# The attention's biases of the first 31 items on GpSimd, with omega scaled as it is loaded

## The chip, the cores and the metric

One core of a Trainium2 chip runs the kernel. The metric is the device time of one execution in microseconds, the median of several runs. The engines are TensorE (PE, with PEld for its weight loads), VectorE (DVE), ScalarE (ACT), GpSimd (POOL) and SyncE (SP), which issues the loads.

## The reference

Three layers follow one another: a linear attention with random features, a two-layer network, and a layer of 8 experts of which each token uses one.

```python
scale = 1.0 / np.sqrt(np.sqrt(D))                  # D = 64
def phi(x):                                        # x = q * scale or k * scale
    proj = np.einsum('bhsd,md->bhsm', x, omega)    # 128 features
    sq = np.sum(x * x, axis=-1, keepdims=True) / 2.0
    h = proj - sq
    h = h - np.max(h, axis=-1, keepdims=True)
    return np.exp(h) / np.sqrt(m)
kv = np.einsum('bhsm,bhsd->bhmd', k_p, v); z = np.sum(k_p, axis=2)
num = np.einsum('bhsm,bhmd->bhsd', q_p, kv)
den = np.einsum('bhsm,bhm->bhs', q_p, z)[..., None] + 1e-06
x = num / den                                      # (4, 8, 576, 64) -> (2304, 512)
h = x @ w_in; y = np.maximum(0.01 * h, h) @ w_out  # 512 -> 2048 -> 512
# experts: argmax of y @ w_gate; relu(y @ w1[e]) @ w2[e], scaled by two gates
```

Everything is float32; the matrix products of the last two layers are made of three products of split numbers.

## The kernel before

The attention's work is cut into 74 items: 36 of keys and 38 of queries, each of four tiles of 128 rows (three in some). An item goes through stages, one per tick of a software pipeline: load, squares, projection, phi, and then either the product with the values (keys) or transposes, the product with the keys' sums, and the division (queries). The list `seq` sets the order of the items; `turn` counts them. The first 13 are 9 items of keys and 4 of queries, with the loading of the first weights between them; the first 31 end with the first queries of the second batch.

From about 50 us on, the two-layer network runs between the stages: for every block of 256 tokens (`c`) and every eighth of the hidden width (`u`) a unit `h_unit` (24 products, lines 463 to 465) and a unit `x_unit` (12 products, lines 482 to 484). Blocks 0 and 1 run side by side. Their weights come as 64-bit words and are turned into float32 on the way (`load_w`, 32 times in the first 170 us): ScalarE takes one part (line 201), VectorE three steps (202 to 204), ScalarE casts the high half (209), GpSimd subtracts for the low half (`wil`, `wol`, line 212). From about 170 us on the weights are resident.

What phi does for one item: TensorE projects into PSUM (`pw`, line 290, with `om_raw`); VectorE takes the maximum `mx` over the 128 features (302, or 304 and 305); `ngm` and `bias` (309, 311) follow on VectorE; ScalarE makes four exponentials (319) with `bias` as their bias. `s2` is half the sum of squares: in 9 items TensorE makes it from `sq` (265, 280), in all others GpSimd squares the rows (`nat`, 270), VectorE sums them (`ssq`, 271) and GpSimd scales them (273). The tiles `mx`, `ngm`, `bias`, `s2` and `ssq` have two buffers each.

```python
ngm = att.tile([P, 4], F32, name="ngm", tag="ngm")
nc.vector.scalar_tensor_tensor(ngm[:, 0:nt], mx[:, 0:nt], -sc, s2[:, 0:nt], op0=ALU.mult, op1=ALU.add)
bias = att.tile([P, 4], F32, name="bias", tag="bias")
nc.vector.tensor_sub(bias[:, 0:nt], ngm[:, 0:nt], s2[:, 0:nt])
```

Each engine runs its instructions in one fixed order. A scheduler sets that order when the program is built, by its own estimates of what each instruction costs, so a change of an engine or an operation can reorder the others around it.

Of the kernel before, what the change touches and what calls it, by code (L numbers as in the profile page):

```python
# [15 lines left out]
AF = mybir.ActivationFunctionType  # L16
ALU = mybir.AluOpType
# [27 lines left out]
WFROM = 0  # L45
WU = 6
TAIL = 9
KQ = 8
WARM = 8
NSLOT = NTOK // SLOT - 1  # L50
# [37 lines left out]
def tile_kernel(ctx: ExitStack, tc: tile.TileContext, kT, k_nat, v_nat, qT, q_nat, om, w_in, w_out, wg, w1, w2, out, stop=None, dbg=None):  # L88
    nc = tc.nc
    sc = 1.0 / math.sqrt(math.sqrt(HD))  # L90
# [44 lines left out]
    with ExitStack() as pa:  # L135
# [9 lines left out]

        om_raw = const.tile([P, 2 * M], F32, name="om_raw")
        nc.sync.dma_start(om_raw, om)
        halves = const.tile([P, 2], F32, name="halves")
        nc.vector.memset(halves, 0.0)
        for i in range(2):  # L150
# [142 lines left out]
        def phi(st, nt):  # L293
            pj = st["pj"]
            if not dense[0] and st["turn"] % 2 == 0:
                h = sb.tile([P, 4, M], F32, name="h", tag="gh")
            else:
                h = att.tile([P, 4, M], F32, name="h", tag="h", bufs=3)
            mx = att.tile([P, 4], F32, name="mx", tag="mx")
            o = mx.rearrange("p (h j) -> p j h", h=2)  # L300
            if nt == 4:
                nc.vector.tensor_reduce(o, pj.rearrange("p (j h) m -> p j h m", h=2), axis=AX.X, op=ALU.max)
            else:
                nc.vector.tensor_reduce(o[:, 0, :], pj[:, 0:2, :], axis=AX.X, op=ALU.max)
                nc.vector.tensor_reduce(o[:, 1, 0:1], pj[:, 2:3, :], axis=AX.X, op=ALU.max)

            s2 = st["s2"]
            ngm = att.tile([P, 4], F32, name="ngm", tag="ngm")
            nc.vector.scalar_tensor_tensor(ngm[:, 0:nt], mx[:, 0:nt], -sc, s2[:, 0:nt], op0=ALU.mult, op1=ALU.add)
            bias = att.tile([P, 4], F32, name="bias", tag="bias")  # L310
            nc.vector.tensor_sub(bias[:, 0:nt], ngm[:, 0:nt], s2[:, 0:nt])  # L311
            st["phi"] = h, pj.rearrange("p (j h) m -> p h j m", h=2), bias
            if st["tight"]:
                phi2(st, nt)

        def phi2(st, nt):
            h, src, bias = st["phi"]
            for j in range(nt):
                nc.scalar.activation(h[:, j, :], src[:, j // 2, j % 2], AF.Exp, bias=bias[:, j:j + 1], scale=sc)  # L319
            st["e"] = h  # L320

        def k_item(b, g):
# [18 lines left out]
            def s_phi():  # L341
                if big:
                    st["vb"] = groups["v", first][:, at - first]
                else:
                    st["vb"] = att.tile([P, 5 * HV], F32, name="vb", tag="vb")
                    n = (5 if any((g * 4 + j) % PT == 0 for j in range(4)) else 4) * HV
                    nc.sync.dma_start(st["vb"][:, 0:n], v_nat[at, :, 0:n])
                phi(st, 4)

            def s_kv():  # L350
                o = 0
                for j in range(4):
# [7 lines left out]
                    if w == PT - 1:  # L360
                        kv_done(b, p)

            st["phi2"] = lambda: phi2(st, 4)
            st["stages"] = [s_load, s_split, s_proj, s_phi, st["phi2"], s_kv]
            return -1, st["stages"]
# [12 lines left out]
        def q_item(b, i, pair0, np_, tile0, at, grp):  # L378
# [16 lines left out]
            def s_phi():  # L395
                phi(st, nt)
# [27 lines left out]
            def s_xt():  # L424
# [18 lines left out]
                if rest_:  # L443
                    o = t[0:HD, np_ * per:np_ * (per + P)].rearrange("p (a k l) -> p a k l", a=np_, k=2)
                    for k in range(2):
                        at = (slice(k * HD, (k + 1) * HD), slice(pair0, pair0 + np_), slice(off + per, off + L))
                        hi_lo(xh[at], xl[at], o[:, :, k, :], nc.scalar, nc.vector)

            st["phi2"] = lambda: phi2(st, nt)
            st["stages"] = [s_load, s_split, s_proj, s_phi, st["phi2"], s_tr, s_num, s_xt]  # L450
            return c, st["stages"]
# [155 lines left out]
        def q_items(b, i):  # L607
            L = pieces(b)[i][1]
            np_ = pairs_of(L)
            first = sum(n for _, n in pieces(b)[:i]) * NH // P  # L610
            at = sum(NH // 2 // pairs_of(n) for c in range(b + 1) for _, n in pieces(c)[:i if c == b else None])
            n = NH // 2 // np_
            return [q_item(b, i, j * np_, np_, first + j * np_ * 2 * L // P, at + j, (at + j // 2 * 2, min(2, n - j // 2 * 2), False)) for j in range(n)]

        def k_items(b, g0, g1):
            return [k_item(b, g) for g in range(g0, g1)]


        seq = k_items(0, 0, KQ) + q_items(0, 0) + k_items(0, KQ, 9)
        first = len(seq)  # L620
# [187 lines left out]
        for i, (c, u) in enumerate(pairs):  # L808

            rate = RATE  # L810
            for cc in range(c, NCH):
                left = [k + TAIL for k, it in enumerate(seq) if it[0] == cc] + [len(o) for c_, o in flow if c_ == cc]
                if left and hbeg.get(cc, 0) - 1 > i:
# [170 lines left out]
```

## Time and profile before

| | us |
|---|---|
| median of 3 runs | 886.59 |
| lowest and highest run | 882.37 and 889.65 |
| the profiled execution | 887.9 |
| its span, first to last instruction | 886.2 |
| TensorE busy in the span | 840.5 |
| VectorE | 449.8 |
| ScalarE | 307.0 |
| GpSimd | 179.5 |

The profile is of one execution. An engine counts as busy while an instruction runs, stalls within it included; a wait for a semaphore counts as idle. TensorE's matmuls overlap, so its busy time is not its best time. PEclk is the share of full clock that the throttle granted.

### The profile page before, as it was taken

To read this page: it belongs to the slowest core of one execution; us is meant where nothing else is said; L and a number is where in the kernel's file an instruction comes from. 1 tells how busy PE (TensorE), PEld (TensorE's weight loads), DVE (VectorE), ACT (ScalarE), POOL (GpSimd) and SP (SyncE) were. 2 spreads that over 40 slices of the span, in tenths; PEclk is the share of its full clock that TensorE was granted. 3 is DMA by queue.
4 is the path that set the end of the run, shared out by engine and by line. 5 is a ranking of instruction groups with operands and counts; after the bars stand their busy time and mean duration, and the time that the engine had idled before them with its cause. 6 is when DMAs were issued, how large, how long until landed. Compare 5 with 4: busy or idle time off the path is not lost. (4 is left out here: it accounts for less than half of the span.)

```text
span 886.2 us, 13999 instructions
## 1 busy us (share of the span) xinstructions
PE 840.5 (95%) x5299; PEld 734.0 (83%) x5299; DVE 449.8 (51%) x1142; ACT 307.0 (35%) x755; POOL 179.5 (20%) x253
## 2 busy tenths in 40 slices
PE   9889998999999999999999999997996999999996
PEld 7768777798899899988889899876886779888894
DVE  6899879626545445445554444454335433512220
ACT  4666655424324224323322232142125432411210
POOL 3545544301221012122010010120013211220001
PEclk9899999999999999999999999999999999999998
DMA  7636554301542021152020000155026622410001
GB/s 225 209 116 192 189 179 138 123 1 31 74 108 78 2 43 53 35 97 60 19 43 6 1 25 1 36 186 72 1 94 208 204 80 98 150 54 21 10 24 33
DMA packets 46153, 73.55 MB, mean 83 GB/s; under 512 B 6017, under 2 KB 28673, under 8 KB 46082
## 3 DMA queue, kind: packets, MB, share of 16 engines
q1 hardware_dynamic: 42562, 63.14, 25.7%
q0 software_dynamic: 3520, 9.47, 3.4%
q8 instruction: 44, 0.72, 0.4%
q14 instruction: 27, 0.22, 0.1%
HBM read 62.00 MB, written 10.59 MB: 82 GB/s over the span
## 5 line engine op out<-in xcount | busy, mean ns | idle before, releaser
L463 PE MATMUL hp<-xh,wih 128*128 128x256 f32 x576 | 167.2, 290 | 2.3 <-DVE xl L212 2.0
L464 PE MATMUL hp<-xl,wih 128*128 128x256 f32 x576 | 162.7, 282 | 0.1
L465 PE MATMUL hp<-xh,wil 128*128 128x256 f32 x576 | 162.1, 281 | 0.0
L482 PE MATMUL acc<-woh,gh 128*128 128x512 f32 x288 | 123.8, 430 | 1.4 <-ACT kv L373 1.4
L484 PE MATMUL acc<-woh,gl 128*128 128x512 f32 x288 | 116.6, 406 | 6.8 <-DVE gl L212 6.8
L319 ACT ACTIVATE h<-pw,bias 128x128 f32<-128x128 f32 x288 | 84.8, 372 | 107.5 <-DVE bias L311 87.7
L469 DVE SCALAR_TENSOR_TENSOR g<-hp,g 128x512 f32<-128x512 f32 x72 | 49.6, 689 | 130.7 <-ACT g L468 118.8
L483 PE MATMUL acc<-wol,gh 128*128 128x512 f32 x288 | 114.8, 399 | 0.0
L463 PEld LDWEIGHTS hp<-xh,wih 128*128 128x128 f32 x576 | 109.7, 190 | 5.5 <-issue 2.4
L464 PEld LDWEIGHTS hp<-xl,wih 128*128 128x128 f32 x576 | 109.6, 190 | 2.2 <-DVE xl L212 0.3
L465 PEld LDWEIGHTS hp<-xh,wil 128*128 128x128 f32 x576 | 109.5, 190 | 0.0
L468 ACT COPY g<-hp 128x512 f32<-128x512 f32 x72 | 42.2, 586 | 134.2 <-PE hp L465 129.6
L713 PE MATMUL eht<-exh,ewh 128*128 128x256 f32 (+1 forms) x256 | 76.9, 301 | 8.9 <-DVE ehl L717 7.2
L714 PE MATMUL eht<-exl,ewh 128*128 128x256 f32 (+1 forms) x256 | 76.4, 298 | 0.4 <-DVE exl L212 0.4
L715 PE MATMUL eht<-exh,ewl 128*128 128x256 f32 (+1 forms) x256 | 76.0, 297 | 0.0
L290 PE MATMUL pw<-om_raw,xpair 128*128 128x256 f32 (+1 forms) x260 | 72.0, 393 | 2.3 <-ACT h L319 2.3
L270 POOL TENSOR_TENSOR nat<-nat 128x256 f32<-128x256 f32 (+1 forms) x65 | 44.8, 692 | 136.8 <-DMA nat<-k_nat 59.0
L484 PEld LDWEIGHTS acc<-woh,gl 128*128 128x128 f32 x288 | 54.9, 191 | 20.5 <-DVE gl L212 8.4
L212 DVE TENSOR_TENSOR ewl<-eraw,ewh 128x1024 fp32r<-128x1024 f32 x32 | 39.1, 1225 | 59.9 <-ACT ewh L209 49.8
L482 PEld LDWEIGHTS acc<-woh,gh 128*128 128x128 f32 x288 | 54.6, 190 | 12.9 <-ACT kv L373 1.8
L730 PE MATMUL eyt<-ewh,ehh 128*128 128x512 f32 (+1 forms) x160 | 64.3, 402 | 0.6 <-ACT ehh L716 0.6
L731 PE MATMUL eyt<-ewl,ehh 128*128 128x512 f32 (+1 forms) x160 | 63.4, 396 | 0.0
(157 smaller groups left out, 1470.9 us busy)
## 6 DMA issues: line engine op xcount, KB each, us to landing
eraw<-w SPq DMA_DIRECT2D x32, 512.0 KB, 4.0
wraw<-w_in SPq DMA_DIRECT2D x16, 512.0 KB, 6.1
wraw<-w_out SPq DMA_DIRECT2D x16, 512.0 KB, 3.4
x_d<-rows SPq DMA_DIRECT2D x9, 514.0 KB
xpair<-qT SPq DMA_DIRECT2D x18, 256.0 KB, 9.0
nat<-q_nat SPq DMA_DIRECT2D x30, 128.0 KB, 2.6
nat<-k_nat SPq DMA_DIRECT2D x27, 128.0 KB, 2.6
xpair<-kT SPq DMA_DIRECT2D x12, 256.0 KB, 3.4
```

What stands on the lines that cost most here:

```text
L290: nc.tensor.matmul(pj[:, 2 * j:2 * j + k // HD, :], st["raw"][0:k, j * P:(j + 1) * P], om_raw[0:k, 0:M * k // HD], start=True, stop=True)
L319: nc.scalar.activation(h[:, j, :], src[:, j // 2, j % 2], AF.Exp, bias=bias[:, j:j + 1], scale=sc)
L463: nc.tensor.matmul(hp[:, i, :], a, xh[:, d, :], start=d == 0, stop=False)
L464: nc.tensor.matmul(hp[:, i, :], a, xl[:, d, :], start=False, stop=False)
L465: nc.tensor.matmul(hp[:, i, :], b_, xh[:, d, :], start=False, stop=d == ND - 1)
L482: nc.tensor.matmul(acc[t], a, h_, start=u == 0 and i == 0, stop=False)
L483: nc.tensor.matmul(acc[t], a, l_, start=False, stop=False)
L484: nc.tensor.matmul(acc[t], b_, h_, start=False, stop=u == NU - 1 and i == 1)
L713: nc.tensor.matmul(t, wh, self.xh[:, d, 0:n], start=d == 0, stop=False)
L714: nc.tensor.matmul(t, wh, self.xl[:, d, 0:n], start=False, stop=False)
L715: nc.tensor.matmul(t, wl, self.xh[:, d, 0:n], start=False, stop=d == ND - 1)
L730: nc.tensor.matmul(t, a, wh, start=f == 0, stop=False)
```

## The change

`om_raw` is multiplied once by the scale, on VectorE, as soon as it has landed. The projections and their maxima then come out scaled, so `ngm` needs no factor: it becomes s2 - mx, a plain subtraction, and the exponentials lose their scale. For the items with `turn` below 31, `ngm` and `bias` are made on GpSimd; for the other 43 they stay on VectorE.

```diff
--- before.py
+++ after.py
@@ -45,6 +45,7 @@
 WFROM = 0
 WU = 6
 TAIL = 9
+EARLY = 31
 KQ = 8
 WARM = 8
 NSLOT = NTOK // SLOT - 1
@@ -145,6 +146,7 @@
 
         om_raw = const.tile([P, 2 * M], F32, name="om_raw")
         nc.sync.dma_start(om_raw, om)
+        nc.vector.tensor_scalar_mul(om_raw, om_raw, sc)
         halves = const.tile([P, 2], F32, name="halves")
         nc.vector.memset(halves, 0.0)
         for i in range(2):
@@ -305,10 +307,11 @@
                 nc.vector.tensor_reduce(o[:, 1, 0:1], pj[:, 2:3, :], axis=AX.X, op=ALU.max)
 
             s2 = st["s2"]
+            eng = nc.gpsimd if st["turn"] < EARLY else nc.vector
             ngm = att.tile([P, 4], F32, name="ngm", tag="ngm")
-            nc.vector.scalar_tensor_tensor(ngm[:, 0:nt], mx[:, 0:nt], -sc, s2[:, 0:nt], op0=ALU.mult, op1=ALU.add)
+            eng.tensor_sub(ngm[:, 0:nt], s2[:, 0:nt], mx[:, 0:nt])
             bias = att.tile([P, 4], F32, name="bias", tag="bias")
-            nc.vector.tensor_sub(bias[:, 0:nt], ngm[:, 0:nt], s2[:, 0:nt])
+            eng.tensor_sub(bias[:, 0:nt], ngm[:, 0:nt], s2[:, 0:nt])
             st["phi"] = h, pj.rearrange("p (j h) m -> p h j m", h=2), bias
             if st["tight"]:
                 phi2(st, nt)
@@ -316,7 +319,7 @@
         def phi2(st, nt):
             h, src, bias = st["phi"]
             for j in range(nt):
-                nc.scalar.activation(h[:, j, :], src[:, j // 2, j % 2], AF.Exp, bias=bias[:, j:j + 1], scale=sc)
+                nc.scalar.activation(h[:, j, :], src[:, j // 2, j % 2], AF.Exp, bias=bias[:, j:j + 1])
             st["e"] = h
 
         def k_item(b, g):
```

In all, 31 pairs leave VectorE for GpSimd, one instruction is added on VectorE, and nothing else changes in number. The order that the scheduler makes changes around them. The names' numbers are one higher in the change, since it has one more instruction.

VectorE, where the first queries' phi begins: `mx_451` is the maximum of an item, `bias_455` its bias; `w32_381` is a weight block in its three steps, `mx_485` and `mx_530` belong to the next two items. Before:

```order
L309 SCALAR_TENSOR_TENSOR ngm_428<-mx_426,s2_352 128x4
L311 TENSOR_TENSOR bias_401<-ngm_399,s2_357 128x4
L202 TENSOR_SCALAR w32_381<-w32_381 128x512
L311 TENSOR_TENSOR bias_430<-ngm_428,s2_352 128x4
L302 TENSOR_REDUCE mx_451<-pw_422 128x2x2
L203 SCALAR_TENSOR_TENSOR w32_381<-wraw_379,w32_381 128x512
L271 TENSOR_REDUCE ssq_417<-nat_415 128x4
L204 SCALAR_TENSOR_TENSOR w32_381<-wraw_379,w32_381 128x512
L309 SCALAR_TENSOR_TENSOR ngm_453<-mx_451,s2_391 128x4
L302 TENSOR_REDUCE mx_485<-pw_447 128x2x2
L271 TENSOR_REDUCE ssq_442<-nat_440 128x4
L311 TENSOR_TENSOR bias_455<-ngm_453,s2_391 128x4
```

After the change, the same stretch:

```order
L273 TENSOR_REDUCE ssq_389<-nat_378 128x4
L304 TENSOR_REDUCE mx_452<-pw_423 128x2x2
L204 TENSOR_SCALAR w32_382<-w32_382 128x512
L273 TENSOR_REDUCE ssq_418<-nat_416 128x4
L205 SCALAR_TENSOR_TENSOR w32_382<-wraw_380,w32_382 128x512
L304 TENSOR_REDUCE mx_486<-pw_448 128x2x2
L206 SCALAR_TENSOR_TENSOR w32_382<-wraw_380,w32_382 128x512
L273 TENSOR_REDUCE ssq_443<-nat_441 128x4
L304 TENSOR_REDUCE mx_531<-pw_482 128x2x2
```

Before, two word steps and a sum stood between the maximum and the first half of its pair, and another maximum and sum before the second half. After, the maxima, sums and word steps follow one another, and the pair (`ngm_454`, `bias_456` of `mx_452`) is gone from this engine.

GpSimd in the same stretch, `wol` being the subtraction for a weight block's low half. Before:

```order
L273 TENSOR_SCALAR s2_352<-ssq_349 128x4
L273 TENSOR_SCALAR s2_391<-ssq_388 128x4
L212 TENSOR_TENSOR wol_309<-w32_311,woh_308 128x512
L270 TENSOR_TENSOR nat_415<-nat_415 128x256
L273 TENSOR_SCALAR s2_420<-ssq_417 128x4
L270 TENSOR_TENSOR nat_440<-nat_440 128x256
L212 TENSOR_TENSOR wol_309<-w32_381,woh_308 128x512
```

After the change:

```order
L275 TENSOR_SCALAR s2_392<-ssq_389 128x4
L272 TENSOR_TENSOR nat_416<-nat_416 128x256
L214 TENSOR_TENSOR wol_310<-w32_312,woh_309 128x512
L312 TENSOR_TENSOR ngm_454<-s2_392,mx_452 128x4
L275 TENSOR_SCALAR s2_421<-ssq_418 128x4
L314 TENSOR_TENSOR bias_456<-ngm_454,s2_392 128x4
L312 TENSOR_TENSOR ngm_488<-s2_421,mx_486 128x4
L272 TENSOR_TENSOR nat_441<-nat_441 128x256
L314 TENSOR_TENSOR bias_490<-ngm_488,s2_421 128x4
L275 TENSOR_SCALAR s2_446<-ssq_443 128x4
```

The pair of `mx_452` stands behind the subtraction of `w32_312`, with a scaling of another item's sums between its two halves; the next pair has a square between its halves and stands ahead of the subtraction of `w32_382`.

GpSimd further on, in the stretch that the trace has at 80 to 91 us. Before:

```order
L273 TENSOR_SCALAR s2_1082<-ssq_1079 128x4
L212 TENSOR_TENSOR wil_1088<-w32_1090,wih_1087 128x512
L273 TENSOR_SCALAR s2_1184<-ssq_1181 128x4
L212 TENSOR_TENSOR wil_1088<-w32_1099,wih_1087 128x512
L273 TENSOR_SCALAR s2_1225<-ssq_1222 128x4
L270 TENSOR_TENSOR nat_1292<-nat_1292 128x256
L270 TENSOR_TENSOR nat_1405<-nat_1405 128x256
L212 TENSOR_TENSOR wol_1108<-w32_1110,woh_1107 128x512
```

After the change:

```order
L275 TENSOR_SCALAR s2_1083<-ssq_1080 128x4
L214 TENSOR_TENSOR wil_1089<-w32_1091,wih_1088 128x512
L312 TENSOR_TENSOR ngm_1171<-s2_1037,mx_1169 128x4
L272 TENSOR_TENSOR nat_1293<-nat_1293 128x256
L314 TENSOR_TENSOR bias_1173<-ngm_1171,s2_1037 128x4
L275 TENSOR_SCALAR s2_1185<-ssq_1182 128x4
L214 TENSOR_TENSOR wil_1089<-w32_1100,wih_1088 128x512
L312 TENSOR_TENSOR ngm_1212<-s2_1083,mx_1210 128x4
L314 TENSOR_TENSOR bias_1214<-ngm_1212,s2_1083 128x4
L275 TENSOR_SCALAR s2_1226<-ssq_1223 128x4
```

Each pair stands behind one subtraction `wil`, the first with a square between its halves, and the scaling that followed the subtraction now follows the pair.

## Rows read from the trace of the kernel before

**Rows 1.** Busy times by stretch: its us, each engine's busy us (instructions), PEclk, DMA

```profile
0.00:170.00 170.00, 151.97 (x925) 128.66 (x926) 140.52 (x325) 98.49 (x254) 82.03 (x106) 0.95 0.57 176
...
170.00:886.00 716.00, 688.51 (x4375) 605.35 (x4373) 309.32 (x817) 208.52 (x503) 97.42 (x147) 0.99 0.23 61
```

**Rows 2.** The same: one slice; four pieces (20:30, 40:70, 80:90, 140:150) summed

```profile
30.00:40.00 10.00, 7.56 (x33) 6.61 (x32) 8.11 (x22) 5.66 (x17) 4.94 (x9) 0.68 0.65 196
...
sum 60.00, PE 52.39 PEld 43.84 DVE 56.34 ACT 39.43 POOL 32.83; mean PE 13.10 PEld 10.96 DVE 14.09 ACT 9.86 POOL 8.21
```

**Rows 3.** TensorE's waits in 0:170: us in total, times, longest

```profile
PE qtp L403 <- ACT h L319: 2.4, 1, 2.4
...
PE pw L290 <- ACT h L319: 2.3, 4, 1.4
...
PE kvp L358 <- ACT h L319: 1.8, 3, 1.0
```

**Rows 4.** What ScalarE waited for in 0:170

```profile
ACT h L319 <- DVE bias L311: 11.8, 10, 2.1
```

**Rows 5.** Lines 309, 311 in 0:170: ns least/median/most, first and last start

```profile
L309 DVE SCALAR_TENSOR_TENSOR ngm<-mx,s x32: 131/155/1198, 7.6 to 166.0; 128x4 f32<-128x4 f32 x28, 128x3 f32<-128x3 f32 x4
...
L311 DVE TENSOR_TENSOR bias<-ngm,s x32: 146/161/1240, 8.8 to 166.9; 128x4 f32<-128x4 f32 x28, 128x3 f32<-128x3 f32 x4
```

**Rows 6.** VectorE, lines 309, 311: sums in 0:170, then in the four pieces

```profile
sum 170.00, DVE 9.63; mean DVE 4.81
...
sum 170.00, DVE 10.71; mean DVE 5.36
...
sum 60.00, DVE 3.92; mean DVE 0.98
...
sum 60.00, DVE 6.16; mean DVE 1.54
```

**Rows 7.** Groups in 0:170: busy us, mean ns (first row: ns least/median/most)

```profile
L273 POOL TENSOR_SCALAR s<-ssq x25: 222/261/643, 25.5 to 167.1; 128x4 f32<-128x4 f32 x21, 128x3 f32<-128x3 f32 x4
...
L212 POOL TENSOR_TENSOR wil<-w,wih 128x512 fp32r<-128x512 f32 x16 | 23.4, 1460 | 20.6 <-ACT wih L209 20.6
...
L270 POOL TENSOR_TENSOR nat<-nat 128x256 f32<-128x256 f32 x24 | 18.4, 770 | 14.4 <-DMA nat<-k_nat 6.5 <-DVE rec L418 2.8 <-DVE gl L212 2.1
...
L273 POOL TENSOR_SCALAR s<-ssq 128x4 f32<-128x4 f32 x21 | 8.1, 384 | 16.5 <-DVE bias L311 9.9 <-DVE ssq L271 5.7 <-DMA nat<-q_nat 0.2
...
L203 DVE SCALAR_TENSOR_TENSOR w<-wraw,w 128x512 int32<-128x512 int32 x32 | 28.3, 885 | 0.1
...
L204 DVE SCALAR_TENSOR_TENSOR w<-wraw,w 128x512 int32<-128x512 int32 x32 | 25.0, 782 | 0.1
```

**Rows 8.** Timeline, 27 to 34 us: start, us, engine, line, out<-in

```profile
27.61 0.68 DVE L302 TENSOR_REDUCE mx<-pw 128x4 f32<-128x512 f32 x1
...
27.78 1.29 POOL L212 TENSOR_TENSOR wol<-w,woh 128x512 fp32r<-128x512 f32 x1
...
31.87 1.26 POOL L212 TENSOR_TENSOR wol<-w,woh 128x512 fp32r<-128x512 f32 x1
...
32.29 0.87 DVE L311 TENSOR_TENSOR bias<-ngm,s 128x4 f32<-128x4 f32 x1
...
33.19 1.14 ACT L319 ACTIVATE h<-pw,bias 128x128 f32<-128x128 f32 x4 [0.91 <-DVE bias L311]
...
33.61 0.47 PE L403 MATMUL qtp<-ident,h 128*128 128x128 f32 x1 [2.44 <-ACT h L319]
```

**Rows 9.** Timeline, 80 to 85 us

```profile
80.21 0.68 DVE L302 TENSOR_REDUCE mx<-pw 128x4 f32<-128x512 f32 x1
...
83.16 1.79 POOL L212 TENSOR_TENSOR wil<-w,wih 128x512 fp32r<-128x512 f32 x1 [2.56 <-ACT wih L209]
...
83.73 1.24 DVE L311 TENSOR_TENSOR bias<-ngm,s 128x4 f32<-128x4 f32 x1
```

**Rows 10.** Timeline, VectorE's first square

```profile
3.36 0.43 DVE L265 TENSOR_TENSOR sq<-xgroup 128x256 f32<-128x256 f32 x1 [2.03 <-DMA xgroup<-kT]
```

## The prediction

> **What bounds the kernel now.** Read the busy times by stretch first. From 170 us on, TensorE is busy 688.5 of 716 us and VectorE 309 [rows 1]: nothing that is taken off VectorE there shortens anything. In the first 170 us TensorE is busy 152.0 and so stands still for 18.0, while VectorE is busy 140.5, GpSimd 82.0 and ScalarE 98.5 [rows 1]. All 31 items that the change touches have their bias in this stretch: 32 of each of the two small instructions lie in it [rows 5], 62 of the 64 being of the first 31 items. The second view narrows it: in four pieces, 60 us together, VectorE is busy 56.3 [rows 2]. There it is the bound, with TensorE at 52.4. TensorE's list of waits says the same: exponentials that came late cost it 2.4 + 2.3 + 1.8 us [rows 3], and ScalarE, which makes the exponentials, waited 11.8 us for the bias in this stretch [rows 4].
>
> The third thing to see is that VectorE's small instructions are half stall. Their median is 0.155 and 0.161 us, their longest 1.198 and 1.240 [rows 5]. Their busy time in 170 us is 9.63 + 10.71 = 20.3 us [rows 6], where 64 at the median would be 10.1. The long ones lie beside a GpSimd instruction: the bias at 83.73 took 1.24 us and ended as GpSimd's subtraction of 83.16 (1.79 us) did, and that at 32.29 took 0.87 beside one of 31.87 [rows 8, 9].
>
> **The change part by part.** I count against the profiled execution, 887.9 us, which is 1.3 above the median of the runs.
>
> Taken off VectorE: 62 of 64 instructions, 62/64 x 20.3 = 19.7 us. Of it 62 x 0.158 = 9.8 us is work that surely leaves. The other 9.9 us is stall, and the GpSimd instruction that caused it is still there: the next VectorE instruction may meet it. Bounds 0 and 9.9; I take half, 4.9, because what follows is often of a kind that I see unhindered (a reduction of 0.68 us at its usual length). Added against it: 62 GpSimd instructions that VectorE can now run into. Nearest row: the scaling of 128x4 on GpSimd, 0.222 us at least, 0.384 on average with its stalls [rows 7]. VectorE's two long word steps alone take 28.3 + 25.0 of 170 us [rows 7], 31%; one that gets ready while GpSimd is at work loses 0.11 on average: 62 x 0.31 x 0.11 = 2.1 us, say 2.8 with its other such instructions (bounds 0 and 62 x 0.222 = 13.8). Net 9.8 + 4.9 - 2.8 = 11.9 us of VectorE's time.
>
> How much reaches the end: in the four pieces where VectorE is the bound lie 3.92 + 6.16 = 10.1 of the 20.3 us [rows 6], one half. Outside it has room, and saved time turns into idle time. So 11.9 x 0.5 = 6 us (bounds 0 and 12).
>
> The place at 33.6 us has a term of its own. TensorE stood still for 2.44 us there, for an exponential that began at 33.19, when the bias was there [rows 8]. The maximum was ready at 28.29, but two word steps, two sums and another maximum stood ahead of the bias, which ended at 33.16. The order of the change puts this bias behind one weight subtraction on GpSimd (27.78 to 29.07 in this trace), a square (0.77 us on average) and three small ones of 0.384 [rows 7], so it ends at about 31: some 2 us sooner, and the next thing that is late is the copy of the transposes behind it. Those microseconds are in the 6 already; the clock is not. TensorE's granted clock in that slice of 10 us is 0.68 [rows 2], so the lower of its two levels (1.2 and 2.4 GHz) stood for most of it, after the engine had been idle; that costs 10 x 0.32 = 3.2 us. I count 2 of it (bounds 0 and 3.2), since another idle stretch may take its place.
>
> GpSimd's queue: 62 x 0.222 to 62 x 0.384, 14 to 24 us, on 82 of 170. GpSimd is not the bound, but the bias now waits for what stands ahead of it in order. Of the 31 pairs, 21 have a weight subtraction (1.46 us [rows 7]) between themselves and the pair before. VectorE's order was no shorter: from the end of the maximum to the end of the bias went 28.29 to 33.16 = 4.9 us and 80.89 to 84.97 = 4.1 us [rows 8, 9]. A full subtraction and two small ones make 1.46 + 2 x 0.384 = 2.2 us. Yet at the second place the change puts subtraction, difference, square and bias in a row: with the subtraction ending at 84.95 as now, the bias would end near 86.5, 1.5 us later than today. ScalarE holds other work there that covers some of it. I take a loss of 1 us in all (bounds 0 and 17, below).
>
> Scaling omega: once, 128x256 on VectorE, 0.43 us by the square of that size, before the first square, for which VectorE stood idle 2.03 us [rows 10]. The load of omega is issued first, so it hides there: 0 (bounds 0 and 0.43; if omega lands after the first keys, all of it shows, since the first projection waits). For items 31 and later a plain subtraction stands in place of a multiply and add: 0.161 against 0.155 us, 0. One queue wait goes: GpSimd's scaling of the next sums waited for VectorE's bias (its buffer has two places). Now both are on GpSimd; it will wait for the maximum instead, and I count 0.
>
> Sum: 887.9 - 6 - 2 + 1 = 880.9, so **881 us**.
>
> A rule speaks against this sum. The trace shows the bias of 1.24 us beside a GpSimd subtraction, eight times its median [rows 5, 9]. The Trainium skill, page "SBUF — State Buffer", section "Who interferes with whom", says that a VectorE instruction with two inputs in SBUF and a GpSimd instruction that reads SBUF shut each other out for a whole instruction; by that rule, the trace agrees, 1.24 against 0.161. It would hand all 9.9 us of stall to the next two-input instruction: 7 us net in place of 11.9, and 883 in place of 881.
>
> **The rivals.** *More than that.* If the stage is set by VectorE from end to end, all 11.9 to 19.7 us come through and the clock with them. TensorE's idle time of 18.0 us and a mean clock of 0.95 over 170 us (8.5 us) [rows 1] leave room. 887.9 - 12 - 3 to - 20 - 3: 865 to 873, with milder forms up to 877. For it: VectorE above 94% in 60 us. Against: TensorE at 87% there.
>
> *The stalls only move.* VectorE keeps the 9.9 us, and each new GpSimd instruction holds it up for its 0.222 us: 9.8 - 13.8, so nothing is won, 886 to 890. The Trainium skill, page "Perfetto Trace Analysis", section "Optimizing Scalar/DVE Operations", warns of just this, that the two share a read port and moving work between them might not help. For it: the long word steps, of one size, average 0.885 and 0.782 us [rows 7], so both kinds are being held up by differing amounts. Against: half the time of the small ones is work, not stall.
>
> *GpSimd's queue becomes the delay, and the kernel slower.* Place: the 21 pairs behind a weight subtraction. Price: half of 1.46 us each on average is 15 us on the exponentials, the whole of it 31. TensorE's waits for exponentials (6.5 us) stand to ScalarE's for the bias (11.8) [rows 3, 4] as 0.55 to 1, so 8 to 17 us. Against the gain of 8 it decides from 0.7 us a pair; at the whole length 887.9 - 8 + 17 = 897. Against: the 4.1 to 4.9 us that the bias waits today.
>
> **How the numbers follow.** My forecast (876 to 885) 0.45; more 0.25 (865 to 877); stalls move 0.19 (885 to 890); slower 0.11 (890 to 900). The bounds of one per cent about 886.6, which is about what a measurement of this kernel can tell, are 877.7 and 895.5. Below lie the second case and a fifth of the first: 0.33. Above lies most of the last: 0.08. Between: 0.59. The range 869 to 892 leaves out the far end of the second case and nearly all of the last, about 0.17.
>
> **What would show it.** Right: in the first 170 us VectorE's busy time falls by 10 to 16 us, its long word steps keep their means, the wait of 2.44 us for the exponential and the low clock after it are gone, TensorE's work of this stretch ends 6 to 9 us sooner, and the rest takes 716 us as before. Stalls moved: the word steps' means rise above 0.9 us. Slower: ScalarE's waits for the bias, now GpSimd's, pass 20 us, and TensorE's for exponentials 10. I am wrong if VectorE's time falls as said and the stage is no shorter: then it was not the bound; or if a new idle stretch of TensorE elsewhere brings the lower clock.

## The result and the profile after

| | before | after |
|---|---|---|
| median, 6 runs each (range), us | 885.6 (882.4 to 889.7) | 898.6 (897.4 to 901.7) |
| ratio (95% interval) | 1 | 1.015 (1.013 to 1.017) |
| profiled execution: time, span, us | 887.9, 886.2 | 901.7, 900.0 |

The kernel is 1.5% slower, outside the range. The busy times by stretch answer to [rows 1, 2]; below them is the slice in which the clock is now low.

```profile
0.00:170.00 170.00, 151.45 (x913) 128.29 (x914) 129.52 (x267) 97.91 (x252) 97.01 (x169) 0.93 0.55 173
170.00:899.00 729.00, 696.01 (x4388) 609.70 (x4387) 307.85 (x815) 208.75 (x503) 96.18 (x147) 0.98 0.23 61
...
40.00:50.00 10.00, 6.39 (x28) 4.64 (x27) 8.27 (x19) 5.45 (x15) 6.04 (x11) 0.75 0.34 90
```

VectorE is 11.0 us less busy in the first 170 us, as forecast, and TensorE did no more work in them. Both lines are cut at 170 us, so the whole difference of the spans stands in the second (716 us, now 729); where it arises is read from the ends of the blocks. The two views of ScalarE's copy that ends each of the nine blocks (kernel after, then before; the last two numbers are the first and the last start) show it.

```profile
L863 ACT COPY rows<-acc x9: 578/587/589, 184.4 to 650.2; 128x512 f32<-128x512 f32 x9
```

```profile
L860 ACT COPY rows<-acc x9: 577/587/592, 181.7 to 637.4; 128x512 f32<-128x512 f32 x9
```

The changed kernel is 2.7 us late at the end of block 0 and 12.8 at the end of the last; from the end of block 0 to the end of the span it takes 715.6 us instead of 704.5. The ends between them put nearly all of that in two steps: 3.7 to 7.6 us late between 334 and 414 us, and 7.9 to 14.5 between 477 and 541. Here is VectorE's timeline in the second step, and TensorE's row behind it:

```profile
520.88 0.69 DVE L472 SCALAR_TENSOR_TENSOR g<-hp,g 128x512 f32<-128x512 f32 x1 [2.62 <-ACT g L471]
528.65 0.42 DVE L213 CAST gh<-g 128x512 fp32r<-128x512 f32 x1 [7.08 <-issue]
528.67 0.06 DVE L862 MEMSET rows<- 128x2 f32 x1
...
529.13 0.50 PE L485 MATMUL acc<-woh,gh 128*128 128x512 f32 x1 [4.04 <-DVE gh L213]
```

TensorE's clock behind it is

```profile
529.00:534.00 5.00, 4.87 (x14) 3.62 (x15) 3.19 (x8) 1.56 (x5) 0.22 (x1) 0.66 0.00 0
```

"issue" says that the profile shows no releaser. In VectorE's own order the memset of `rows` stands between `g` and `gh`: it writes the buffer from which the last block's rows are stored, and so waits for the end of that store. In the kernel before the same three stand close together:

```profile
512.25 0.69 DVE L469 SCALAR_TENSOR_TENSOR g<-hp,g 128x512 f32<-128x512 f32 x1 [2.62 <-ACT g L468]
512.89 0.06 DVE L859 MEMSET rows<- 128x2 f32 x1
512.98 0.43 DVE L211 CAST gh<-g 128x512 fp32r<-128x512 f32 x1
```

What differs is in the DMA queues while that store's packets are under way: 518.8 to 521.6 us after the change, 510.2 to 512.0 before it (the share is of the 16 DMA engines).

```profile
q1 hardware_dynamic: 272, 0.53, 50.8%
q14 instruction: 1, 0.01, 1.7%
```

```profile
q1 hardware_dynamic: 272, 0.53, 78.8%
```

After the change a fetch of instructions (a transfer that brings an engine its next instructions) falls into the store. In the first step VectorE stands 8.2 us at such a memset up to 396.6 us, and TensorE's rows behind it, then its clock in 400 to 405 us, are

```profile
398.46 1.16 PE L361 MATMUL kvp<-vb,h 128*128 128x66 f32 x8 [1.33 <-DMA vb<-v_nat]
...
400.80 1.95 PE L292 MATMUL pw<-om_raw,xpair 128*128 128x256 f32 x4 [1.18 <-ACT h L322]
...
400.00:405.00 5.00, 4.20 (x10) 2.85 (x11) 2.68 (x8) 2.58 (x9) 0.85 (x2) 0.50 0.33 86
```

The kernel before has such a wait there too, with one TensorE pause of 1.0 us behind it and a granted clock of 1.00 from 385 to 405 us:

```profile
391.59 0.69 DVE L469 SCALAR_TENSOR_TENSOR g<-hp,g 128x512 f32<-128x512 f32 x1 [6.81 <-issue]
391.61 0.06 DVE L859 MEMSET rows<- 128x2 f32 x1
```

A granted clock of 0.50 is the lower of the two levels, 1.2 GHz. The fetches tell another story here than in the second step. These are the ones around that store, in the kernel before (381 to 393 us) and after the change (384.5 to 397):

```profile
q8 instruction: 1, 0.02, 0.5%
...
q14 instruction: 1, 0.01, 0.2%
```

```profile
q8 instruction: 1, 0.02, 0.9%
```

The one of 16 KB (q8) begins at nearly the same place of TensorE's list in these two profiles and in the five of the next section that still have this wait (behind 2335 to 2355 of its recorded matmuls), so it is TensorE's. The one of 8 KB (q14) is VectorE's: it is gone where VectorE's list is 61 instructions shorter, and there again where 63 copies make up for them (next section). So the kernel before has two fetches at this store, and the change took VectorE's away from it. The wait became longer all the same, 8.2 us instead of 6.8.

In the first 170 us ScalarE, TensorE and VectorE wait as follows (total, times, longest), which answers to [rows 3, 4]; the second line is the kernel before's, a wait that [rows 4] leave out:

```profile
ACT h L322 <- POOL bias L314: 34.5, 16, 7.5
```

```profile
ACT h L319 <- DVE ngm L309: 7.1, 1, 7.1
```

```profile
PE pw L292 <- ACT h L322: 4.1, 4, 1.7
PE kvp L361 <- ACT h L322: 3.0, 3, 1.7
PE acc L485 <- ACT h L322: 2.5, 1, 2.5
PE qtp L406 <- ACT h L322: 1.9, 1, 1.9
```

```profile
DVE ssq L273 <- POOL s L275: 10.6, 11, 3.1
DVE mx L304 <- PE pw L292: 6.5, 7, 1.7
```

ScalarE's waits for the pair went from 11.8 + 7.1 = 18.9 us to 34.5, and TensorE's for exponentials from 6.5 to 11.5. VectorE now waits 10.6 us for GpSimd where it waited 2.3. The two long word steps average 926 and 779 ns against 885 and 782 [rows 7], and the pair on GpSimd (the two lines of [rows 5]) is now

```profile
L312 POOL TENSOR_TENSOR ngm<-s,mx x31: 189/203/671, 7.0 to 147.2; 128x4 f32<-128x4 f32 x27, 128x3 f32<-128x3 f32 x4
...
L314 POOL TENSOR_TENSOR bias<-ngm,s x31: 193/198/702, 9.5 to 147.9; 128x4 f32<-128x4 f32 x27, 128x3 f32<-128x3 f32 x4
```

### The profile page after: what moved, and what is told of

Read it like the earlier page. It is cut to its first block, busy times and chain, and to the rows that moved or that the text cites. A ratio compares the mean times of both kernels' runs of the same rounds, so it can differ in the third digit from the quotient of the medians.

```text
span 900.0 us, 14005 instructions
## 1 busy us (share of the span) xinstructions
PE 847.5 (94%) x5299; PEld 738.0 (82%) x5299; DVE 437.4 (49%) x1081; ACT 306.7 (34%) x755; POOL 193.2 (21%) x315
## 5 line engine op out<-in xcount | busy, mean ns | idle before, releaser
L485 PE MATMUL acc<-woh,gh 128*128 128x512 f32 x288 | 126.0, 438 | 6.9 <-DVE gh L213 4.0
L487 PE MATMUL acc<-woh,gl 128*128 128x512 f32 x288 | 119.2, 415 | 6.1 <-DVE gl L214 6.1
L486 PE MATMUL acc<-wol,gh 128*128 128x512 f32 x288 | 118.1, 410 | 0.0
L485 PEld LDWEIGHTS acc<-woh,gh 128*128 128x128 f32 x288 | 56.8, 197 | 19.8 <-DVE gh L213 4.7
L486 PEld LDWEIGHTS acc<-wol,gh 128*128 128x128 f32 x288 | 56.4, 196 | 10.4
## 6 DMA issues: line engine op xcount, KB each, us to landing
eraw<-w SPq DMA_DIRECT2D x32, 512.0 KB, 3.8
wraw<-w_in SPq DMA_DIRECT2D x16, 512.0 KB, 8.7
wraw<-w_out SPq DMA_DIRECT2D x16, 512.0 KB
```

The source lines that it names most:

```text
L485: nc.tensor.matmul(acc[t], a, h_, start=u == 0 and i == 0, stop=False)
L486: nc.tensor.matmul(acc[t], a, l_, start=False, stop=False)
L487: nc.tensor.matmul(acc[t], b_, h_, start=False, stop=u == NU - 1 and i == 1)
```

## The experiments

Ratios are to the kernel before, timed on the same chip, with their 95% intervals; 0.1% is 0.9 us. The profiled executions of one kernel differ by some microseconds, so sizes are taken from ratios, and profiles are read for where things wait.

**The late loss: waits for stores.** Theory F in the expectations says that VectorE's list is shorter by 61 instructions (62 gone, one added), so that its fetches come at other places and meet a store. The changed kernel once more:

> The changed kernel once more, beside the others. Theory F: the places of fetches and stores don't change from one execution to the next, so VectorE's waits of 7 to 9 us at 385 to 400 and of 6 to 8 us at 520 to 530 are there again: 1.012 to 1.018 of before. If they were accidents of one execution: 1.003 to 1.009.

1.0149 (1.0093 to 1.0204). VectorE's waits at the two memsets were 8.18 us (385.4 to 393.6) and 7.11 (518.2 to 525.4). They belong to the program, not to one execution.

Scaling and plain subtractions alone, `EARLY` set so that no pair moves:

```diff
-EARLY = 31
+EARLY = 0
```

> Only half of the change: omega scaled once, plain subtractions, no scale in the exponentials, but every pair stays on VectorE. Theory F (the late loss comes from VectorE's list being 62 instructions shorter, so that instruction fetches fall at other points and meet the store of a block's rows; the early loss from GpSimd's queue): VectorE's list is one longer than before, both causes are absent, 883 to 889 us, the copies that end block 0 at 181 to 183 us. Rival S (the plain subtraction or the exponential without a scale costs time everywhere): 890 to 899. Rival Q (GpSimd's queue is the whole loss): 883 to 889 as well.

1.0002 (0.9972 to 1.0031), the longest wait at a memset 4.9 us near 381, none near 506. Rival S falls: this half of the change costs nothing that shows.

Copies on VectorE that do nothing useful, behind the end of block 0, in the changed kernel (63) and in the kernel before (65). VectorE's order is otherwise the same row for row, and so is that of the other engines.

```diff
             nc.vector.tensor_copy(rows[:, 1, 0:D], acc[c][1])
+            if c == 0:
+                for _ in range(63):
+                    nc.vector.tensor_copy(combo, rows[:, 1, 0:1])
```

> The kernel before with 65 such copies after block 0, so that VectorE's list from there on is 128 longer than that of the changed kernel, one fetch more. Theory F: nothing is on GpSimd, yet the late loss of the changed kernel appears: 892 to 898 us, with a wait of VectorE of some 7 us at 510 to 520 us ahead of the memset of the rows. Rival Q: 885 to 889, no such wait.

> The changed kernel with 63 copies of 128x1 on VectorE that read block 0's rows and write a scratch column, between 185 and 215 us, where VectorE has room; every other instruction stands as in the changed kernel. Theory F: from there on fetches fall where they fell before, so only the early loss of 2.7 us stays: 888 to 891 us, and the wait of 7.1 us of VectorE at about 521 us is gone. Rival Q (the queue, the exponentials and the clock carry the loss): the copies change nothing, 897 to 901.

The kernel before with 65 copies: 1.0096 (1.0069 to 1.0122), 8.5 us. Its VectorE timeline now has the wait of the changed kernel, without any change of the pairs:

```profile
509.42 0.69 DVE L469 SCALAR_TENSOR_TENSOR g<-hp,g 128x512 f32<-128x512 f32 x1 [2.62 <-ACT g L468]
516.94 0.42 DVE L211 CAST gh<-g 128x512 fp32r<-128x512 f32 x1 [6.82 <-issue]
516.96 0.06 DVE L859 MEMSET rows<- 128x2 f32 x1
```

The changed kernel with 63: 1.0089 (1.0059 to 1.0120), and there the wait is gone:

```profile
514.37 0.69 DVE L472 SCALAR_TENSOR_TENSOR g<-hp,g 128x512 f32<-128x512 f32 x1 [2.62 <-ACT g L471]
515.01 0.06 DVE L862 MEMSET rows<- 128x2 f32 x1
515.10 0.43 DVE L213 CAST gh<-g 128x512 fp32r<-128x512 f32 x1
```

So at this place the number of VectorE's instructions ahead of it decides, as theory F said. The size of the second run was forecast too low (1.003 to 1.006), since the wait near 385 us stayed (7.5 us).

The rows of blocks 3 and 5 in another buffer:

```diff
-            rows = (wst if c == 1 else rt).tile([P, 2, ROW], F32, ...
+            rows = (wst if c == 1 else sb if c in (3, 5) else rt).tile([P, 2, ROW], F32, ...
```

> The changed kernel with the rows of blocks 3 and 5 in a second place in memory, so that the memset of the next block's rows doesn't wait for the store of the last ones; the fetches stay where they are. Theory F: the waits of VectorE of 8.2 us at 388 us and of 7.1 us at 521 us are gone, and with them the late loss and what the first of them costs the kernel before too: 884 to 890 us. A rival, that the fetch itself starves VectorE and the store has no part in it: VectorE still stands still for some 7 us at about 521 us, 896 to 901.

1.0089 (1.0060 to 1.0118), neither of the two. The fetch still falls into the store at 511.4 to 513.5 us, but no memset waits for that store now, and VectorE runs on: `gh` starts at 514.08, right behind `g`. So the fetch doesn't starve VectorE; it is the store's end that comes late. The wait near 385 us is still there (7.1 us), because the scheduler put the memset of block 5 where that of block 4 had been. The edit removed one wait of two.

Over the seven profiles that still have the waiting memset (before, after, and the five runs above), the nine stores that a fetch met and that a memset waited for were followed by it 2.7 to 7.6 us after the last packet. Of the 39 others (three of them with a fetch that began as the last packet ended), 37 were followed 1.0 to 2.1 us after it, one, in the kernel before, 3.4, and one 6.4. That last one is the store near 380 us in the kernel with 65 copies: no fetch lies between its first packet and its last (TensorE's begins 0.07 us behind it), and yet VectorE waits 5.4 us there. At that place the wait is long in all seven, 4.9 to 8.2 us, with VectorE's fetch in the store (before, scaling alone, 63 copies: 6.8, 4.9 and 7.5) and without it (8.2, 8.2, 7.1 and 5.4). What makes that store's end late isn't settled, and neither is why the wait is longer with the pairs on GpSimd (7.1 to 8.2) than without (4.9 to 6.8). With them there TensorE's fetch begins between 0.4 us before and 0.9 us after the store's first packet, in the others 1.7 to 2.0 us after it; no run tests whether that is the reason.

No wait for a store at all: the zero is made from the block's sums at its end.

```diff
-            nc.vector.memset(rows[:, :, D + 1:D + 2], 0.0)
...
             nc.vector.tensor_copy(rows[:, 1, 0:D], acc[c][1])
+            for t in range(2):
+                nc.vector.tensor_scalar(rows[:, t, D + 1:D + 2], acc[c][t][:, 0:1], 0.0, 0.0, op0=ALU.mult, op1=ALU.add)
```

> The kernel before, but the zero in the last column of a block's rows is made from the block's sums at its end (two VectorE instructions of 128x1) and no longer by a memset that waits for the store of the block before. Theory F: VectorE has no wait at 381 us any more; TensorE's idle microsecond behind it goes, 0.997 to 1.000 of before. A rival, that VectorE's waits there come from its own instruction fetch: a wait of 5 to 8 us at about 381 us stays.

> The changed kernel with the same edit. Theory F: both waits (8.2 us at 388, 7.1 us at 521) and the low clock behind them are gone, and what is left is the early loss: 2 to 5 us more than the kernel before with this edit, 1.000 to 1.004 of before. Rival Q (the early queue and what follows from it is the whole loss): 1.010 to 1.016 of before.

0.9999 (0.9974 to 1.0023) and 1.0040 (1.0019 to 1.0060), with none of VectorE's waits at a memset in either. So 1.0150 - 1.0040 = 1.1%, 9.7 us, are the waits for stores; the same wait of 6.8 us in the kernel before was covered and cost nothing. By the run with 63 copies 5.4 us belong to the place at 521 (1.0150 - 1.0089) and 4.3 to that near 388, each give or take some 3 us; the kernel before with 65 copies puts 8.5 on the first of the two. All further kernels have this edit, the "late zero".

**The early loss: 0.4%.** Since s2 - mx - s2 is -mx but for the rounding, a bias can be had without a pair. Without the pairs of the first 31 items (omega is scaled by -sc, the maximum becomes a minimum, and the exponentials get a scale of -1):

```diff
-        nc.vector.tensor_scalar_mul(om_raw, om_raw, sc)
+        nc.vector.tensor_scalar_mul(om_raw, om_raw, -sc)
...
+            bias = mx
+            if st["turn"] >= EARLY:
...
```

> With the same edit, and for the first 31 items neither VectorE nor GpSimd makes the pair: omega is scaled by -sc, the maximum is taken as a minimum, and that is the bias (the rounding of the difference with the squares is left out for these items). So 62 instructions leave VectorE and none is added anywhere. If the first stage hangs on VectorE's time, as the prediction had it, its end comes 5 to 9 us sooner than in the kernel before with this edit: 0.988 to 0.994 of before. If it does not: 0.996 to 1.000. In both, TensorE's waits for exponentials in the first 185 us fall below the 6.5 us of before.

0.9949 (0.9921 to 0.9978), 4.5 us, between the two forecasts. So the pairs do cost time in the first stage, but all that they cost, their wait before an exponential included, is 4.5 us (2 to 7). TensorE's waits for exponentials in 185 us came to 7.6 us, not below 6.5.

All pairs on VectorE (`EARLY = 0`), and those of the first 31 items a second time on GpSimd, for nobody:

```diff
...
+            if st["turn"] < 31:
...
+                nc.gpsimd.tensor_sub(ngd[:, 0:nt], s2[:, 0:nt], mx[:, 0:nt])
...
+                nc.gpsimd.tensor_sub(bid[:, 0:nt], ngd[:, 0:nt], s2[:, 0:nt])
```

> With the same edit and all pairs on VectorE, as in the kernel that only scales omega; GpSimd makes the pairs of the first 31 items a second time, into tiles that nobody reads. If the early loss comes from GpSimd's added instructions as such (the shared port, GpSimd's queue in front of the squares and weights): 2 to 5 us over the kernel before with this edit, 1.000 to 1.004. If it comes from the exponentials' wait for a bias that stands in GpSimd's queue: 0.996 to 1.000.

1.0013 (0.9992 to 1.0034). That lies in the range of the first theory, but the interval holds both nothing at all and most of the 3.5 us, so this run doesn't decide between the two. Against the gain of 4.5 the move's price on GpSimd is 3.5 + 4.5 = 8.0 us, give or take 3. Taken as it stands, the run puts some 1.2 us of it on GpSimd's added instructions as such, and some 6.8 would be left for the waits for these biases. One place in the changed kernel with the late zero shows such a wait (GpSimd's rows, then VectorE's, ScalarE's and TensorE's):

```profile
109.15 1.76 POOL L214 TENSOR_TENSOR wol<-w,woh 128x512 fp32r<-128x512 f32 x1 [2.67 <-ACT woh L211]
110.87 0.50 POOL L272 TENSOR_TENSOR nat<-nat 128x192 f32<-128x192 f32 x1
111.34 1.29 POOL L214 TENSOR_TENSOR wol<-w,woh 128x512 fp32r<-128x512 f32 x1
112.60 0.19 POOL L312 TENSOR_TENSOR ngm<-s,mx 128x4 f32<-128x4 f32 x1
112.87 0.20 POOL L314 TENSOR_TENSOR bias<-ngm,s 128x4 f32<-128x4 f32 x1
113.16 0.24 POOL L275 TENSOR_SCALAR s<-ssq 128x3 f32<-128x3 f32 x1
```

```profile
109.66 0.68 DVE L304 TENSOR_REDUCE mx<-pw 128x4 f32<-128x512 f32 x1
113.42 0.35 DVE L273 TENSOR_REDUCE ssq<-nat 128x3 f32<-128x192 f32 x1 [3.08 <-POOL s L275]
```

```profile
113.10 1.14 ACT L322 ACTIVATE h<-pw,bias 128x128 f32<-128x128 f32 x4 [2.71 <-POOL bias L314]
```

```profile
114.30 1.13 PE L292 MATMUL pw<-om_raw,xpair 128*128 128x256 f32 x4 [1.35 <-ACT h L322]
```

The maximum ended at 110.34. GpSimd had two weight subtractions and a square ahead of the pair, the first of them late because it waited for ScalarE; so the bias came at 113.07, and until then VectorE, ScalarE and at last TensorE stood still. Before the change VectorE would have made the pair itself and gone on.

Is it the weight subtractions? Both kernels without them, so that the low halves of the weights are left out of the result:

```diff
-            hi_lo(wh, wl, w.bitcast(F32), nc.scalar, nc.gpsimd)
+            nc.scalar.copy(wh, w.bitcast(F32))
...
```

> A control: the kernel before with the late zero, and without the subtractions that make the low halves of the weights on GpSimd (1.4 us each in the first stage); the products that take a low half take the high half in its place, so that part of the result's accuracy is left out and TensorE's work stays the same. GpSimd is busy some 40 us less in the first 185 us; VectorE's long word steps meet it less. Both theories: 0.985 to 0.999 of before; it is the base for the next run.

> The changed kernel with the same two edits, so that nothing long stands ahead of the pairs in GpSimd's queue. Theory Q (the early loss is the pairs' wait behind weight subtractions): the move now pays, 2 to 6 us less than the control without weight subtractions, and ScalarE's wait for a bias falls from 37 us to under 22. A rival, that the price lies in handing the maximum from VectorE to GpSimd and on to ScalarE, and in GpSimd's slower instructions: the loss stays, 1 to 5 us more than the control.

0.9892 (0.9829 to 0.9955) and 0.9874 (0.9826 to 0.9923). ScalarE's wait for GpSimd's bias fell from 37 to 21 us, and the loss is no longer to be seen; but a gain of 2 us or more, as expected, isn't shown either with these intervals, and in the two profiles the move still ends block 0 2.8 us later. Inconclusive.

Four places for the sums of squares instead of two:

```diff
-            ssq = att.tile([P, 4], F32, name="ssq", tag="ssq")
+            ssq = att.tile([P, 4], F32, name="ssq", tag="ssq", bufs=4)
```

> The changed kernel with the late zero and four places instead of two for the sums of squares that VectorE makes and GpSimd scales; the order of GpSimd's and TensorE's work is as good as unchanged. Theory L (lockstep: VectorE, which gave up the pairs, now waits for GpSimd to have read an old sum of squares, 10.9 us against 2.3, because GpSimd's queue holds the pair and a weight subtraction ahead of that read, and the word steps behind VectorE's wait feed ScalarE and GpSimd again): the wait falls below 4 us and the early loss goes, 0.996 to 1.001 of before. Rival P (the bias as such comes later because of its place in GpSimd's queue): the wait falls, but the time stays at 1.002 to 1.006.

> The control: the kernel before with the late zero and four places for the sums of squares. VectorE's wait for these is 2.3 us there: 0.997 to 1.002 of before by either theory.

1.0056 (1.0035 to 1.0077) and 1.0027 (1.0006 to 1.0049), the control a little slower than both theories had it (1.002 at most). VectorE's wait fell only from 10.9 to 8.0 us, and a difference of 0.3% stayed. That the two places make the wait and the loss, as theory L had it, is refuted.

The pairs with a higher priority in the scheduler (the two subtractions stand under the `with`):

```diff
...
+            with tc.high_priority(offset=AHEAD if st["turn"] < EARLY else 0):
...
```

> The changed kernel with the late zero, and the pairs on GpSimd given the priority that the block's products have, so that they come ahead of squares and weight subtractions in GpSimd's queue where the two are due at about the same time. Rival P: the early loss goes, 0.995 to 1.000 of before. Theory L: the pair waits for the maximum at the head of the queue, and what stands behind it waits with it: 1.002 to 1.008.

1.0041 (1.0014 to 1.0069): as without it. But GpSimd's order hardly changed: 19 of the 31 pairs still have a weight subtraction between themselves and the pair before (21 without the priority), and from 80 us on it is much the same. So the run doesn't tell whether bringing the pairs forward would help.

The pairs of the first 20 items alone, and those of items 20 to 30 alone:

```diff
-            eng = nc.gpsimd if st["turn"] < EARLY else nc.vector
+            eng = nc.gpsimd if 20 <= st["turn"] < EARLY else nc.vector
```

> The changed kernel with the late zero and only the first 20 items' pairs on GpSimd (their biases end before 80 us); the other 11 are on VectorE as before. Theory W (the loss is made between 80 and 135 us, where weight subtractions stand densest in GpSimd's queue ahead of pairs and VectorE waits 7.5 us behind them; until 80 us the move wins): 0.995 to 1.000 of before. Rival H (the price is the same for every pair, being the way from VectorE to GpSimd and on to ScalarE): two thirds of the loss stay, 1.002 to 1.004.

> The other part alone: the pairs of items 20 to 30 on GpSimd, the first 20 on VectorE. Theory W: all of the loss and none of the gain, 1.003 to 1.008 of before, with VectorE's wait of over 5 us for the sums of squares between 80 and 135 us. Rival H: a third of the loss, 1.000 to 1.002.

1.0023 (0.9996 to 1.0050) and 1.0069 (1.0046 to 1.0093). The 11 pairs from 80 us on make at least the whole loss; by them a price that is the same for each pair is refuted, though the run with the first 20 lies where rival H had it. That the first 20 gain, as theory W had it, isn't shown.

Last, no pair for any item:

> The pair is left out for all items, with the late zero: the bias is the minimum itself (the rounding of the difference with the squares is left out). What is won in the first stage should stay as without the pairs of the first 31 items, 0.995 of before; behind it TensorE is the bound and nothing more is won: 0.991 to 0.998.

0.9920 (0.9895 to 0.9946), 881.0 against 887.6 us: the fastest kernel of this study with the full work of TensorE, and faster than both.

## Why the prediction was wrong

**The step that failed most** is "the rest takes 716 us as before", with the 0 for items 31 and later. It looked at what the later instructions do and not at where they lie in VectorE's list. Waits of a memset for two stores took 9.7 of the 13.3 us in its place. At the store near 519 us the cause is shown: 61 instructions fewer moved one of VectorE's fetches into it (5.4 us; 8.5 in the kernel before with 65 copies). At the one near 385 us the wait grew from 6.8 to 8.2 us and was no longer covered; VectorE's fetch had left that store, and the cause is open. Nothing in the rows that I had chosen shows it; the trace of before did show a wait of 6.8 us that nobody releases, in front of such a memset.

**The second** is the term "I take a loss of 1 us in all (bounds 0 and 17)" for GpSimd's queue. It came to 8.0, give or take 3. I argued from two places where the bias waited 4.1 and 4.9 us on VectorE. Matching the n-th maximum with the n-th bias over all 31 items gives 2.7 us from one end to the other, 83.9 in all, so the two were not typical. After the change it is 61.6: the bias comes sooner on average, by 0.7 us, and yet the stage gets longer. So the wait per pair was the wrong quantity to price. The traces suggest why, though no run isolates it: while VectorE held a bias back it made the word steps that ScalarE and GpSimd needed next; now, where a pair is late on GpSimd, VectorE stands as well. Its waits for GpSimd at the sums of squares grew by 8.3 us (2.3 to 10.6), and the 11.0 us of work that it gave up became idle time.

**What held.** VectorE's net relief was put at 11.9 and measured 11.0. The Trainium skill, page "SBUF — State Buffer", section "Who interferes with whom", says that a VectorE instruction with two inputs in SBUF contends with a GpSimd instruction that reads SBUF. The prediction's estimate from it, that the whole stall passes to the next such instruction, gave 7; the 11.0 speak against the whole of it. One word step's mean rose past the 0.9 us that the prediction named as a sign of stalls that only move (0.885 to 0.926), the other stayed, and together the 64 steps took 1.2 us more, far from that rival's size. The 62 instructions took 19.1 us on GpSimd (11.7 and 7.4; 14 to 24 forecast), and the scaling of omega cost nothing that the run with it alone shows. The gain of 6 and 2 us from VectorE's relief is bounded by the run without pairs, 4.5: right in sign, too large. The pause of 2.44 us at 33.6 is gone, but another of 1.9 at 45.7, behind one of 1.4 at 42.5, took its place and the low clock with it (0.75 in 40 to 50 us against 0.68 in 30 to 40 [rows 2]), so the clock's 2 us were not won. I had named that.

**The rivals.** The one with GpSimd's queue gave 897 us with both its signs (ScalarE's waits for a bias 34.5, over 20; TensorE's for exponentials 11.5, over 10), and the median is 898.6. That is no confirmation: its mechanism made 3.5 us of net loss, and the rest came from the stores.

**Open.** What holds up the end of the store near 385 us, in both kernels, isn't known. Why the wait there costs 4.3 us and the one of 6.8 us before nothing is read only from the profiles: two pauses of 1.33 and 1.18 us instead of one of 1.00, and then the low clock. Which of GpSimd's other instructions, besides the weight subtractions, hold up the pairs after 80 us isn't settled, nor whether an earlier place in GpSimd's queue would help.

## What to carry to other kernels

An edit that only removes instructions from an engine also moves everything behind them in its list: check, before trusting a stage that "is not touched", which waits there are released by a DMA and are only just covered. Work taken off a busy in-order engine can be lost again in the new owner's queue; price it where the queue is longest, and ask who else stands while it waits. A write that needs an old store to be done belongs where it is needed, not as early as the scheduler can put it.

## What the runs showed of the hardware

An instruction fetch that falls into a store of 514 KB can go with a late end of that store: the last packet to the waiting memset took 2.7 to 7.6 us in nine such cases, against 1.0 to 2.1 in 37 of 39 others. At the place near 519 us the two go together when VectorE's list is moved: 63 idle copies took fetch and wait away, and 65 in the kernel before brought both. At the place near 385 us they don't: the wait was 5.4 us with no fetch inside the store. The fetch itself is small (in those cases 8 KB in 0.3 to 0.8 us, or 16 KB in 0.9 to 1.9). In the changed kernel ScalarE's fetches come after 188, 316, 446, 573 and 703 of its recorded instructions, one in 127 to 130, and VectorE's on either side of 385 us after 561 and 688, so 61 instructions are half such a step. What holds the end back inside the DMA isn't shown.

The Trainium skill, page "Runtime: NRT & Kernel Launch", section "Instruction fetch mechanics", says that the cost of crossing a block is mostly hidden; here the engine itself was not starved, as it says, but the way round through the store near 519 us cost 5.4 and 8.5 us by the two runs with copies. Its page "DMA: Bandwidth & Descriptors", section "Anatomy of one DMA — SWDGE (gpsimd) path", says of transfers that GpSimd issues that the wait until the last write is confirmed can be surprisingly long when HBM is written. These stores are issued by SyncE; that their up to 7.6 us are such a wait no run here shows.
